# Copying and storing the last left-over rows of a fused attention and feed-forward kernel: two engines with half the columns each, and two stores of 64 rows in place of four of 32

## The chip, the cores and the metric

The kernel runs on one core of one Trainium2 chip. The metric is the device time of one execution in microseconds (us), as a median over runs. A core has a matrix engine (PE, with its weight loads as PEld), VectorE (DVE), ScalarE (ACT), GpSimd (POOL) and SyncE (SP). Transfers between the core's memory and the chip's main memory are issued from an engine's instruction queue and carried out by 16 DMA engines.

## The reference

Eight batches, 8 heads, 576 tokens, head size 64, 32 memory slots; the tokens then go through two dense layers with an ELU between them.

```python
a = exp(phi - max(phi, axis=2)); a = a / (sum(a, axis=2) + 1e-9)
k_m = einsum('bhsm,bhsd->bhmd', a, k)          # 32 slots per head
v_m = einsum('bhsm,bhsd->bhmd', a, v)
attn = softmax(q @ k_m.T / 8)                   # over the 32 slots
x = (attn @ v_m) as [4608 tokens, 512]
h = x @ w_in                                    # 512 -> 2048
g = where(h > 0, h, exp(min(h, 0)) - 1)
out = g @ w_out                                 # 2048 -> 512, all float32
```

## The kernel before

Batches are worked on one after another; a batch's 576 tokens are cut into two halves of 288. The first dense layer (`hidden`, L776) makes, for one of 16 blocks of 128 hidden channels, the channels of one half. ScalarE and VectorE apply the ELU and split the result into a high and a low part. The second layer (`project`, matmuls at L837) multiplies these parts with the weights and sums them in accumulators of 128 tokens by 512 outputs, one bank each (`pso...`).

288 tokens are two full tiles of 128 and 32 left over. The left-over tokens of the two halves of two batches, 4 x 32 = 128, are gathered in tiles called `rest` and go through the second layer together, once for every pair of batches: `rest_high` (ScalarE, L881), `rest_low` (VectorE, L886) and `rest_project` (matmuls, L837), eight steps each. There are four pairs, so this happens four times, and the fourth time is the end of the program.

The order of the work is an explicit list of steps with places; at the end of the last batch the list reads: the last `project`, the eight steps of the left-over tokens with the last two full tiles copied out by `collect` (ScalarE L867, VectorE L869) between them, `store` of these two full tiles (issued on SP, L872), and then `rest_store` of the fourth pair, to which nothing comes after. In `rest_store` ScalarE copies the accumulator of 128 rows by 512 outputs into a tile `orest` (L900), and four transfers bring its rows to the output (L904). Row `n * 32 + i` of the tile is left-over token `i` of batch `2p + n // 2`, half `n % 2`. For the fourth pair the transfers are issued from SP (n = 0 and 2) and from ScalarE's queue (n = 1 and 3). The output is laid out as batch, half, token in half, 512 numbers; the left-over tokens of one half are 32 neighbouring rows there, and those of the next half begin 288 rows further on.

The two full tiles of a half are stored by one transfer whose loops are 128 rows, 2 tiles and 512 numbers (256 rows of 2 KB); a store of left-over rows before has loops of 32 rows and 512 numbers (32 rows of 2 KB).

Of the kernel before, what the change touches and what calls it, by code (L numbers as in the profile page):

```python
# [16 lines left out]
P = 128  # L17
B, H, S, D, M = 8, 8, 576, 64, 32
DM, DFF = 512, 2048
HALF = S // 2  # L20
NT = HALF // P
REST = HALF - NT * P
# [146 lines left out]
def fused_kernel(ctx: ExitStack, tc: tile.TileContext, phiT, phi, kv0, kvt, kv, q0, q1, w_in, w_out, out):  # L169
# [8 lines left out]
    nc = tc.nc  # L178
# [13 lines left out]
    def t2k(shape, name):  # L192
        return work.tile(shape, F32, name=name, tag="t2k", bufs=7)
# [638 lines left out]
    acc = {}  # L832
# [64 lines left out]

    def rest_store(p):
        t = t2k([P, DM], "orest")
        nc.scalar.copy(t, acc.pop(("rest", p)))  # L900

        eng = (nc.sync, nc.scalar) if p == B // 2 - 1 else (nc.sync, nc.sync)
        for n in range(4):
            eng[n % 2].dma_start(  # L904
                out[2 * p + n // 2, n % 2, NT * P :], t[n * REST : (n + 1) * REST, :]
            )

    tiny = work.tile([P, 1], F32, name="tiny", bufs=1)
    warm = ps_o.tile([P, P], F32, name="pso00")
# [4 lines left out]
    def warm_up(n):  # L914
# [8 lines left out]
        for f in (  # L923
# [4 lines left out]
            softmax_divide, back, turn_back, probs_high, probs_low, vw, vw_high, vw_low, hidden,  # L928
            elu_exp, elu_max, elu_rest, rest_copy, elu_high, elu_low, project, collect, store, rest_high, rest_low,
            rest_project, rest_store,  # L930
        )
    }
# [67 lines left out]
    for it, (b, hf, j) in enumerate(order):  # L1000
        at(it - 1.7, hidden, it)
        at(it - 1.69, elu_exp, it)
        at(it - 1.68, elu_max, it)
        if b < NB:
            at(it - 1.67, rest_copy, it)
        elif b > NB and b % 2 == 0 and order[max(it - 2, 0)][0] != b:
            at(32 * b - 0.34 + 0.005 * (it - 32 * b), elu_rest, it)
        else:
            at(it - 1.67, elu_rest, it)
        late = 0.695 if it and b != order[it - 1][0] and b % 2 == 0 and b > NB else 0  # L1010
        at(it - 1 + late, elu_high, it)
        at(it - 0.99 + late, elu_low, it)
        at(it + 0.6, project, it)
        if ends[it][2]:
            for t in range(NT):
                at(it + 0.7, collect, it, t)
            if j == NJ - 1:
                at(it + 0.8, store, b, hf)
                if b % 2 and hf:
                    for i in range(NJ // 2):  # L1020
                        at(it + 0.61 + 0.01 * i, rest_high, b // 2, i)
                        at(it + 0.611 + 0.01 * i, rest_low, b // 2, i)
                        at(it + 0.612 + 0.01 * i, rest_project, b // 2, i)
                    at(it + 0.81, rest_store, b // 2)
# [51 lines left out]
```

## Time and profile before

| what | value |
|---|---|
| median of 3 runs | 713.0 us (712.86 to 714.35) |
| the profiled execution's own time | 713.61 us |
| its span, first to last instruction | 711.8 us |
| PE busy in the span | 700.6 us (98%) |
| DVE busy | 449.1 us (63%) |
| ACT busy | 458.9 us (64%) |
| written to main memory | 9.44 MB |

The span is what the trace sees; the execution's own time is 1.8 us longer. The share of busy time of an engine says how full it is over the whole span, not which engine sets the end: that is read from the chain of work that ended last, and from the last few us in order of time.

### The profile page before, as it was taken

The numbers are of one execution on the slowest core, as the hardware profiler recorded it, in microseconds if no ns is written. First come the engines' busy times: TensorE is split into PE (matmuls) and PEld (weight loads), VectorE is DVE, ScalarE is ACT, GpSimd is POOL, SyncE is SP. The second block draws the span as 40 slices with busy tenths as digits, with TensorE's granted clock in tenths as the row PEclk, the third lists the DMA queues.
The fourth block names the chain that finished last, engine by engine and source line by source line (L and its number), as shares of the span: only waits on it lengthen the run. The fifth ranks groups of instructions, "written<-read, shape, count | busy, mean of one in ns | idle before, by whom it ended". The sixth has DMA issues, their size and how long they took to land.

```text
span 711.8 us, 13641 instructions
## 1 busy us (share of the span) xinstructions
PE 700.6 (98%) x5112; PEld 581.9 (82%) x5112; DVE 449.1 (63%) x1197; ACT 458.9 (64%) x1106; POOL 67.5 (9%) x110
## 2 busy tenths in 40 slices
PE   8899999999999999999999999999999999999997
PEld 7788787878777887788787887888878788778886
DVE  3989788876685459563863638754683546944442
ACT  3888988886456556574664845765574655756652
POOL 1233321323000100010000100001000020000000
PEclk9999999999999999999999999999999999999999
DMA  8991012342303600262003620135001450000001
GB/s 330 407 380 61 1 60 89 112 160 48 134 36 85 200 30 2 97 163 76 1 1 111 164 76 1 49 106 151 31 1 45 92 184 31 1 31 1 29 1 46
DMA packets 25106, 64.46 MB, mean 91 GB/s; under 512 B 3408, under 2 KB 7632, under 8 KB 25040
## 3 DMA queue, kind: packets, MB, share of 16 engines
q1 hardware_dynamic: 24944, 63.46, 27.5%
q8 instruction: 41, 0.67, 0.4%
q14 instruction: 25, 0.20, 0.1%
q10 hardware_dynamic: 96, 0.13, 0.1%
HBM read 54.13 MB, written 9.44 MB: 89 GB/s over the span
## 4 chain that ended last, share of the span: by engine, by line
PE 94%; DVE 2%; DMA 1%; ACT 1%; SPq 1%; issue 0%
PE pso L837 56%; PE psh L776 29%; PE psb L554 4%; PE psb L487 2%; PE pso L554 2%; DMA qh<-q 1%; PE pso L567 1%; PE psb L567 0%; SPq L309 0%; ACT gf L792 0%; PE psb L523 0%; DVE gf L800 0%; ACT gf L791 0%; DVE mx L612 0%; DVE A L713 0%; DVE spare L628 0%
## 5 line engine op out<-in xcount | busy, mean ns | idle before, releaser
L837 PE MATMUL pso<-wout,gp 128*128 128x512 f32 x1728 | 441.0, 395 | 0.5 <-ACT orest L900 0.5
L837 PEld LDWEIGHTS pso<-wout,gp 128*128 128x128 f32 x1728 | 310.7, 188 | 62.4 <-ACT gf L792 2.4
L776 PEld LDWEIGHTS psh<-A,vw 128*128 128x128 f32 x1536 | 227.4, 188 | 36.8 <-issue 11.6
L776 PE MATMUL psh<-A,vw 128*128 128x288 f32 x1536 | 246.5, 297 | 2.2 <-DVE A L713 0.8
L803 DVE SCALAR_TENSOR_TENSOR gf<-gf,psh 128x256 f32<-128x256 f32 x192 | 80.7, 420 | 143.5 <-ACT gf L792 143.3
L791 ACT ACTIVATE gf<-psh 128x288 f32<-128x288 f32 x256 | 104.6, 409 | 103.2 <-PE psh L776 102.3
L823 ACT CAST gp<-gf 128x256 fp32r<-128x256 f32 x256 | 102.9, 404 | 78.2 <-DVE gf L803 66.0
L829 DVE TENSOR_TENSOR gp<-gf,gp 128x256 fp32r<-128x256 f32 x256 | 110.9, 436 | 49.7 <-ACT gp L823 48.6
L792 ACT ACTIVATE gf<-gf 128x288 f32<-128x288 f32 x256 | 113.9, 445 | 8.1
L285 POOL TENSOR_TENSOR e<-e,nmb 128x512 f32<-128x512 f32 (+1 forms) x18 | 21.1, 1198 | 366.5 <-DMA nmb<-nmd 280.6
L800 DVE SCALAR_TENSOR_TENSOR gf<-gf,psh 128x288 f32<-128x288 f32 x64 | 28.6, 451 | 22.0 <-ACT gf L792 21.0
L811 DVE SCALAR_TENSOR_TENSOR rest<-gf,psh 128x32 f32<-128x32 f32 x192 | 34.7, 181 | 0.0
L738 DVE TENSOR_TENSOR vw<-psb,vw 128x512 fp32r<-128x512 f32 (+2 forms) x48 | 27.0, 586 | 3.7 <-ACT vw L732 3.7
L881 ACT CAST gp<-rest 128x256 fp32r<-128x256 f32 x32 | 12.6, 405 | 23.7 <-PE pso L837 23.7
L819 POOL COPY rest<-gf 128x32 f32<-128x32 f32 x64 | 19.1, 329 | 74.0 <-DVE gf L800 73.9
L732 ACT CAST vw<-psb 128x512 fp32r<-128x512 f32 (+2 forms) x48 | 22.5, 497 | 2.5 <-PE psb L554 2.4
L886 DVE TENSOR_TENSOR gp<-rest,gp 128x256 fp32r<-128x256 f32 x32 | 13.0, 418 | 16.3 <-ACT gp L881 16.3
L554 PE MATMUL psb<-win,kvm 64*32 64x512 f32 (+2 forms) x384 | 22.3, 521 | 0.0
L383 ACT ACTIVATE mag<-raw 128x512 uint32<-128x512 uint32 x30 | 19.9, 669 | 1.7 <-DVE top L405 1.7
L379 ACT ACTIVATE mag<-raw 128x512 f32<-128x512 f32 x30 | 19.9, 668 | 0.0
L738 DVE TENSOR_TENSOR vw<-pso,vw 128x512 fp32r<-128x512 f32 (+1 forms) x28 | 17.3, 626 | 0.0
L487 PE MATMUL psb<-kvt,e 128*32 128x128 f32 (+1 forms) x480 | 15.1, 274 | 0.0
(133 smaller groups left out, 438.1 us busy)
## 6 DMA issues: line engine op xcount, KB each, us to landing
kvt<-kv SPq DMA_DIRECT2D x32, 512.0 KB, 7.5
raw<-w_in SPq DMA_DIRECT2D x15, 512.0 KB, 9.9
raw<-w_out SPq DMA_DIRECT2D x15, 512.0 KB, 4.2
out<-osb SPq DMA_DIRECT2D x14, 512.0 KB, 2.8
qt<-q SPq DMA_DIRECT2D x18, 384.0 KB, 4.1
ph<-phiT SPq DMA_DIRECT2D x7, 576.0 KB, 4.6
e<-phi SPq DMA_DIRECT2D x12, 256.0 KB, 4.7
kvt<-kv SPq DMA_DIRECT2D x6, 256.0 KB, 10.0
```

Of the source, the lines that this page charges most:

```text
L487: nc.tensor.matmul((ps[a] if b < NB else ps[:, a])[32 * j : 32 * j + 32], s["e"][c // 2][rows, c % 2, x : x + M], kv_rows(b, c, i, 2 * j + a),
L554: nc.tensor.matmul(outs[a][32 * j : 32 * j + 32, :], lhs[r, 32 * j : 32 * j + 32], rhs[r, j], start=True, stop=True, tile_position=(64 * a ...
L738: nc.vector.tensor_tensor(t[:, LO, a, n0:n1], s["ps"]["vw", c, n0][a], t[:, HI, a, n0:n1], ALU.subtract)
L776: nc.tensor.matmul(ps, t[:, x, g, c0 : c0 + P], s["A"][hf][:, y, g, :], start=(n == 0), stop=(n == 5),)
L791: nc.scalar.activation(gf, ps, AF.Relu, scale=-1.0)
L792: nc.scalar.activation(gf, gf, AF.Exp, scale=-1.0)
L800: nc.vector.scalar_tensor_tensor(gf, gf, -1.0, ps, ALU.add, ALU.max)
L803: nc.vector.scalar_tensor_tensor(gf[:, :n], gf[:, :n], -1.0, ps[:, :n], ALU.add, ALU.max)
L811: nc.vector.scalar_tensor_tensor(rest_of(b, j)[:, o : o + REST], gf[:, n:], -1.0, ps[:, n:], ALU.add, ALU.max)
L823: nc.scalar.copy(gp[:, HI], gs[it][:, : NT * P])
L829: eng.tensor_tensor(gp[:, LO], gf[:, : NT * P], gp[:, HI], ALU.subtract)
L837: nc.tensor.matmul(ps, gp[:, y], wout[j][:, x, :], start=(first and n == 0), stop=(last and n == 2),)
```

## The change

Only the fourth `rest_store` is changed; the first three pairs keep one copy on ScalarE and four transfers on SP. For the fourth pair ScalarE copies columns 0 to 255 of the accumulator and VectorE columns 256 to 511, and two transfers follow, one from SP with the rows of batch 6 and one from ScalarE's queue with those of batch 7. Each takes 64 rows of the tile and writes them as 2 halves by 32 rows by 512 numbers.

```diff
     def rest_store(p):
         t = t2k([P, DM], "orest")
-        nc.scalar.copy(t, acc.pop(("rest", p)))
-
-        eng = (nc.sync, nc.scalar) if p == B // 2 - 1 else (nc.sync, nc.sync)
-        for n in range(4):
-            eng[n % 2].dma_start(
-                out[2 * p + n // 2, n % 2, NT * P :], t[n * REST : (n + 1) * REST, :]
-            )
+        ps = acc.pop(("rest", p))
+        if p < B // 2 - 1:
+            nc.scalar.copy(t, ps)
+            for n in range(4):
+                nc.sync.dma_start(
+                    out[2 * p + n // 2, n % 2, NT * P :], t[n * REST : (n + 1) * REST, :]
+                )
+            return
+        nc.scalar.copy(t[:, : DM // 2], ps[:, : DM // 2])
+        nc.vector.tensor_copy(t[:, DM // 2 :], ps[:, DM // 2 :])
+        for n, eng in enumerate((nc.sync, nc.scalar)):
+            eng.dma_start(out[2 * p + n, :, NT * P :], t[n * 2 * REST : (n + 1) * 2 * REST, :])
```

How the instructions stand on ScalarE at the end of the program, lines of before with a minus and of the change with a plus. In brackets are the counters that an instruction waits for: those of PE, DVE and Activation (ScalarE) count finished work of that engine, and DMAHW0 to DMAHW7 count transfers.

```order
 L881 CAST gp<-rest 128x256 [waits DVE_49,PE_49] x6
 L867 COPY osb<-pso_7875 128x512 [waits DMAHW6_49]
-L900 COPY orest<-pso_8174 128x512 [waits PE_49]
-L904 DMA out<-orest 32x512 [waits DMAHW1_49,Activation_49]
-L904 DMA out<-orest 32x512 [waits DMAHW3_49]
-L1071 UNCONDITIONAL_BRANCH
+L908 COPY orest<-pso_8174 128x256 [waits PE_49]
+L911 DMA out<-orest 2x32x512 [waits DMAHW1_49,DVE_49]
+L1076 UNCONDITIONAL_BRANCH
```

The copy has half the columns, one transfer of loops 2 x 32 x 512 stands where two of 32 x 512 stood, and it waits for VectorE's counter and no longer for ScalarE's own.

On VectorE, at the end of the program:

```order
 L886 TENSOR_TENSOR gp<-rest,gp 128x256 [waits Activation_49] x8
 L869 COPY osb<-pso_7876 128x512 [waits DMAHW6_49]
-L1071 UNCONDITIONAL_BRANCH
+L909 COPY orest<-pso_8174 128x256 [waits Activation_49]
+L1076 UNCONDITIONAL_BRANCH
```

VectorE's copy is new there, and it waits for ScalarE's counter, not for PE's. The value that it waits for is the count that ScalarE reaches with its own half of the copy.

On SP, at the end of the program:

```order
 L872 DMA out<-osb 128x2x512 [waits DMAHW7_49,DVE_49,Activation_49]
 L872 DMA out<-osb 128x2x512 [waits DMAHW0_49,DVE_49,Activation_49]
-L904 DMA out<-orest 32x512 [waits DMAHW2_49,Activation_49]
-L904 DMA out<-orest 32x512 [waits DMAHW4_49]
-L1071 UNCONDITIONAL_BRANCH
+L911 DMA out<-orest 2x32x512 [waits DMAHW2_49,DVE_49]
+L1076 UNCONDITIONAL_BRANCH
```

SP issues one transfer after VectorE's copy where it issued two after ScalarE's. The loops shown are those of the written side; on the side of the tile the transfer has one loop of 64 rows.

## Rows read from the trace of the kernel before

**Rows 1.** The page: the span, the busy time of each engine with its share and count of instructions, and, in 40 equal slices of the span, the busy tenths of PE and the granted clock of TensorE in tenths.

```profile
span 711.8 us, 13641 instructions
PE 700.6 (98%) x5112; PEld 581.9 (82%) x5112; DVE 449.1 (63%) x1197; ACT 458.9 (64%) x1106; POOL 67.5 (9%) x110
...
PE   8899999999999999999999999999999999999997
...
PEclk9999999999999999999999999999999999999999
```

**Rows 2.** The chain of work that ended last, the pieces from 690 us on, in order of time: start us, us, what.

```profile
692.57 15.09 PE pso L837 x66
707.65 0.02 issue
707.68 0.58 ACT orest L900
```

**Rows 3.** The instructions from 705 us to the end in order of time: start us, us, engine (SPq and ACTq are the instruction queues, where transfers are issued), line, operation, tiles, count, and in brackets the idle time before it and what ended it.

```profile
704.32 0.68 DVE L869 COPY osb<-pso 128x512 f32<-128x512 f32 x1
704.71 2.93 PE L837 MATMUL pso<-wout,gp 128*128 128x512 f32 x12
...
705.07 0.37 SPq L872 DMA_DIRECT2D out<-osb  x1
707.68 0.58 ACT L900 COPY orest<-pso 128x512 f32<-128x512 f32 x1 [3.25 <-PE pso L837]
708.29 0.80 SPq L904 DMA_DIRECT2D out<-orest  x2
708.29 0.87 ACTq L904 DMA_DIRECT2D out<-orest  x2
```

**Rows 4.** Who waited for whom on SP's queue from 690 us on: us in total, times, longest. L1071 is the end of the program.

```profile
SPq L1071 <- DMA out<-orest: 1.6, 1, 1.6
```

**Rows 5.** Groups of instructions by line and shape, whole span: line, engine, operation, out<-in, shapes and count, then busy us, mean ns of one, and idle us before them. Copies out of an accumulator bank with 512 and with 256 columns, on ScalarE and on VectorE.

```profile
L900 ACT COPY orest<-pso 128x512 f32<-128x512 f32 x4 | 2.3, 582 | 7.0 <-PE pso L837 7.0
L532 ACT COPY kvm<-psb 128x256 f32<-128x256 f32 x6 | 2.1, 358 | 1.4 <-PE psb L523 1.4
L471 ACT COPY win<-pso 128x256 f32<-128x256 f32 x1 | 0.4, 354 | 0.0
L471 DVE COPY spare<-psb 128x256 f32<-128x256 f32 x1 | 0.4, 424 | 0.5 <-PE psb L462 0.5
```

**Rows 6.** Instructions around 703.5 us in order of time, columns as in rows 3: a VectorE instruction that waits for one of ScalarE.

```profile
703.53 0.41 ACT L881 CAST gp<-rest 128x256 fp32r<-128x256 f32 x1 [0.98 <-PE pso L837]
...
703.98 0.42 DVE L886 TENSOR_TENSOR gp<-rest,gp 128x256 fp32r<-128x256 f32 x1 [0.96 <-ACT gp L881]
```

**Rows 7.** The transfer issues on SP around 398.4 and 399 us, columns as in rows 3. The first row is two loads of 128 rows of 4 KB, the second is one of 128 rows and one of 64 rows.

```profile
398.36 0.86 SPq L299 DMA_DIRECT2D kvt<-kv  x2
...
398.84 1.02 SPq L299 DMA_DIRECT2D kvt<-kv  x2
```

**Rows 8.** DMA traffic from 709 to 709.44 us: the busy share in tenths of the 16 DMA engines, in 40 slices of 0.011 us, and the packets of each queue (q1 holds the transfers issued on SP, q10 those issued on ScalarE's queue): packets, MB, share.

```profile
DMA  0000000000099908605970990099998000740609
...
q1 hardware_dynamic: 35, 0.06, 59.1%
q10 hardware_dynamic: 1, 0.00, 2.0%
```

**Rows 9.** DMA traffic from 710 us to the end of the span, in 40 slices of 0.05 us: busy tenths of the 16 engines.

```profile
DMA  9595100000000000000000000000000000000000
```

**Rows 10.** DMA traffic from 705.5 to 708 us, in which only the store of the two full tiles (L872, 256 rows of 2 KB) runs: packets, MB; then how many of them are under 512 bytes, under 2 KB and under 8 KB.

```profile
DMA packets 272, 0.52 MB, mean 210 GB/s; under 512 B 16, under 2 KB 16, under 8 KB 272
```

**Rows 11.** DMA traffic from 709 to 710.5 us, in which only the four stores of left-over rows (L904, 32 rows of 2 KB each, two from each queue) run.

```profile
DMA packets 192, 0.26 MB, mean 175 GB/s; under 512 B 64, under 2 KB 64, under 8 KB 192
...
q10 hardware_dynamic: 96, 0.13, 37.9%
q1 hardware_dynamic: 96, 0.13, 29.9%
```

**Rows 12.** Three stretches: us, busy time of PE, PEld, DVE, ACT and POOL, granted TensorE clock, mean busy share of the 16 DMA engines, GB/s. The first lies in the store of the two full tiles, the second and third in the stores of left-over rows.

```profile
706.40:706.90 0.50, 0.50 (x4) 0.41 (x3) 0.00 (x0) 0.00 (x0) 0.00 (x0) 1.00 0.98 389
709.40:709.70 0.30, 0.00 (x0) 0.00 (x0) 0.00 (x0) 0.00 (x0) 0.00 (x0) 1.00 1.02 219
709.70:710.00 0.30, 0.00 (x0) 0.00 (x0) 0.00 (x0) 0.00 (x0) 0.00 (x0) 1.00 0.91 308
```

## The prediction

> **What bounds the kernel now.** I read the page first. PE is busy for 98% of the span at full granted clock [rows 1], so nothing that another engine saves counts before PE's last matmul. The edit lies wholly behind that matmul. The second view is therefore the chain that ended last, in order of time: a run of matmuls up to 707.65 us, then ScalarE's copy of the left-over accumulator [rows 2], to which no other work runs beside on PE, DVE or ACT [rows 3]. From there on everything is serial and uncovered: copy, issue, transfer, end of program. A us gained or lost in it is a us of the kernel.
>
> The third view is the end in order of time. The copy ends at 707.68 + 0.58 = 708.26; both queues begin to issue at 708.29, two transfers each [rows 3]. The first data of SP's transfers moves at 709.12 (the twelfth slice of 0.011 us) and ScalarE's at 709.44, where its queue has one packet [rows 8]: 0.83 and 1.15 us after the issue began. The last data is through at 710.3 [rows 9]. The wait that ends last is SP's, at the end of the program, for these stores [rows 4]. From the last data to the end of the span, 711.8 - 710.3 = 1.5 us go into the landing's report and the closing of the program. So the tail of 4.15 us behind PE is: copy 0.6, issue to first data 0.85, data 1.2, closing 1.5.
>
> **The change, part by part.**
>
> The copy. ScalarE's half is the same operation as the 256-column copies out of a bank, 0.354 to 0.358 us [rows 5], so it ends at 707.68 + 0.36 = 708.04. VectorE's half doesn't run beside it: as it stands on its queue it waits for ScalarE's count, not PE's. Such a handover takes 703.98 - 703.94 = 0.04 us [rows 6]. VectorE's 256-column copy is 0.424 us [rows 5], so it ends at 708.04 + 0.04 + 0.42 = 708.50, where before the whole copy was done at 708.26. Halved and serial, the copy costs 0.24 us more. Nothing is queued behind the waiting copy but the end of the program; both stores wait for it. Were the halves side by side, they would end at 707.68 + 0.42 = 708.10, 0.16 us sooner than before.
>
> The issues. Each queue now issues once. Before, the second issue of a queue went on while the data of the first was on its way, so removing it takes at most the 0.4 us by which it stood behind the first [rows 3]. The new issue has a form that the trace doesn't show; the nearest is a 64-row load on SP, which took 0.16 us longer to issue than a 128-row one (1.02 for the pair against 0.86) [rows 7]. I take 0.15, with 0 and 0.3 as ends. First data: SP 708.52 + 0.83 + 0.15 = 709.50, ScalarE's queue 708.52 + 1.15 + 0.15 = 709.82.
>
> The data. The bytes are the same, 128 rows of 2 KB. What is in question is over how many DMA engines they are dealt. The trace allows a count: a transfer leaves small packets of a few bytes behind its rows, 272 - 256 = 16 for the store of the full tiles [rows 10], and 192 - 128 = 64 for the four stores of 32 rows [rows 11], 16 for each. With 16 engines on the core the plain reading is one for each engine that took part. So stores whose outer loop has 128 or 32 steps on both sides, each divisible by 16, were dealt over all 16. The new store has an outer loop of 2 on the written side and of 64 on the tile's side; the pieces that both have in common are 2, each of 32 rows. If work is dealt out by pieces of the outer loops, each store runs on 2 engines. No row of this trace has such a pair of loops, so both ends must be kept: 16 engines, or 2. I take 2, since in each store counted the outer loops match and divide by 16, and here they do neither. The Trainium skill, DMA: Bandwidth & Descriptors, section on why a DMA increments its semaphore by 16, gives the count as the largest up to 16 that divides the slowest dimension of both sides, and says that such a transfer takes the lowest-numbered engines; it would be 2 here, the same two for both stores. The trace agrees as far as its 16 small packets go, and no run so far shows a smaller count.
>
> With the same two engines for both stores, each has 64 rows, one after another. The price of a row on one engine is read from the rate and the share [rows 12]. In the store of the full tiles 389 GB/s at a share of 0.98 is 24.8 GB/s for a busy engine: 83 ns for 2 KB. In the stores of left-over rows it was 219 GB/s at 1.02, 13.4 GB/s, 153 ns, while both queues were at rows of the first half of the tile, and 308 at 0.91, 21.2 GB/s, 97 ns, once rows of the other half joined in. Ends: 64 x 83 = 5.3 us and 64 x 153 = 9.8 us. The new stores have rows of the first half on SP and of the second on ScalarE's queue, both at once, and are nearest to the third stretch: 64 x 97 = 6.2 us. The Trainium skill, SBUF, section Door 1, has a reason for the slow rate: partitions p and p + 32 share a port, so a transfer from partitions 0 to 63 has half the ports; that would put the two engines of one store on one port, and by its 27.2 GB/s a port I'd estimate 4.8 us with two ports always busy and 9.6 us with one.
>
> **The sum.** The data runs from 709.50 to 709.50 + 6.2 = 715.7, where it ended at 710.3: +5.4 us. Copy and issue are in that start. The closing 1.5 us stays. The span becomes 711.8 + 5.4 = 717.2 and the profiled execution's own time 713.61 + 5.4 = 719.0. It was 0.6 above the median of the runs, so for the median I take 713.0 + 5.4 = 718.4 us. With the ends of the row's price: +4.5 (717.5) and +9.0 (722.0).
>
> **The rivals.**
>
> *Sixteen engines anyway (not slower).* The hardware may see that 2 x 32 rows on the written side are the 64 on the tile's side and deal by rows. Then each engine has 8 rows: 4 from 709.50 on and 4 from 709.82 on, done between 709.82 + 4 x 0.097 = 710.2 and 709.50 + 8 x 0.153 = 710.7, against 710.3: -0.1 to +0.4 us, and the time is 713.0 to 713.4. The saved issue and the serial copy cancel. For it: every transfer counted so far used all 16; against it: each had matching outer loops. It decides wherever a store is dealt over 8 engines or more: at 8 the data is 16 x 0.097 = 1.6 us, and the loss 0.8 us.
>
> *Two engines, other ones for each store.* Then an engine has 32 rows, from 709.82 on for the later store: 32 x 0.083 to 32 x 0.153 is 2.7 to 4.9 us, ending at 712.5 to 714.7: +2.2 to +4.4 us, 715.2 to 717.4. Both queues reaching all 16 engines in the stores before (16 small packets for each) speaks against it.
>
> *The two engines in step.* If both keep to the same half of the tile at any moment, the slow stretch's 153 ns holds throughout: +9.0, 722.0 us. For it: both engines start one store together. Against: two queues feed each engine, and in the third stretch mixed rows came at 97 ns.
>
> *Faster.* What the edit can save at all is 0.16 us of copy if the halves ran together and 0.4 of issue, 0.6 us or 0.08%; it can't reach the 0.2% below.
>
> **How the numbers follow.** The measurement tells from no change what differs by more than about 0.2%, 1.4 us. Chances: 0.55 for two shared engines near the row's middle price, 0.18 for them in step, 0.08 for separate pairs, 0.17 for sixteen engines, 0.02 for gains that I see no source of. Slower: 0.55 + 0.18 + 0.08 = 0.81; same 0.17; faster 0.02. The range takes in the first three cases, 0.81: from 715.2 (separate pairs at the lowest price) to 722.0 + 0.3 for the issue + 0.3 for spread between runs, 722.6. The likeliest case's own range is 717.2 to 720.
>
> **What would show it.** The chain to PE's last matmul is as before and ends near 707.7. VectorE's L909 starts about 0.04 us behind ScalarE's L908, which takes 0.36. Both queues issue once, near 708.5. In the stretch of the stores the small packets number 4 and not 32, DMA's share is about 2/16 = 0.12 and the rate 40 to 50 GB/s, for 6 us. SP's wait for the stores, 1.6 us before, grows to some 7. It is wrong if 32 small packets show, if the share stands at 0.8 or more, or if the data is through before 711 us.

## The result and the profile after

| what | before | change |
|---|---|---|
| median of 5 runs | 713.14 us | 721.03 us (719.86 to 722.44) |
| ratio, with its 95% interval | 1 | 1.0087 (1.0063 to 1.0111) |
| span of the profiled execution | 711.8 us | 720.7 us |
| from the end of PE's last matmul to the end of the span ("the tail") | 4.15 us | 10.8 us |

The change makes the kernel slower by 0.87%, or 6.2 us by the ratio; the range ran from 715.2 to 722.6 us, and the forecast was 718.4. The two medians lie further apart, 7.9 us, and PE doesn't end at the same time in every execution, as two profiles of the change below show; the tail leaves that out.

The end of the chain that ended last, in the profile of the change (start us, us, what), answers to [rows 2]:

```profile
694.79 15.09 PE pso L837 x66
709.87 0.02 issue
709.89 0.38 ACT orest L908
710.28 0.02 issue
710.30 0.42 DVE orest L909
```

PE's last 66 matmuls take the same 15.09 us, and VectorE's half of the copy follows ScalarE's. PE ends at 709.87 where it ended at 707.65, 2.2 us later. That part isn't the edit's, as the lines below say (busy times of the engines from 20 to 40 us, then the granted clock, the DMA share and the rate; first this profile, with five of these 20 us by themselves, then a second one of the same kernel, from the last run below).

```profile
20.00:40.00 20.00, 18.39 (x191) 15.78 (x192) 16.54 (x41) 15.35 (x36) 4.62 (x3) 0.83 1.02 406
25.00:30.00 5.00, 5.00 (x44) 4.33 (x44) 3.65 (x10) 3.32 (x9) 2.84 (x2) 0.50 1.03 407
```

```profile
20.00:40.00 20.00, 18.19 (x235) 14.88 (x233) 19.08 (x47) 17.66 (x44) 5.04 (x5) 1.00 1.02 406
```

In the first profile TensorE's granted clock was 0.83 in the mean of this stretch and 0.50 from 25 to 30 us, which is 1.2 GHz in place of 2.4, some 670 us ahead of the edit. In the second it had the full clock, PE ended at 707.83, and the span was 718.6: 6.8 us over that of before, nearly all of it tail. So all profiles below are compared by their tails.

The issues of the change, in order of time (columns as in [rows 3]):

```profile
710.75 0.67 SPq L911 DMA_DIRECT2D out<-orest  x1
710.76 1.38 ACTq L911 DMA_DIRECT2D out<-orest  x1
```

DMA traffic of the change from 711 us to the end (packets, MB; then those under 512 bytes, 2 KB and 8 KB; then the two queues), which answers to [rows 11]:

```profile
DMA packets 132, 0.26 MB, mean 27 GB/s; under 512 B 4, under 2 KB 4, under 8 KB 132
...
q1 hardware_dynamic: 66, 0.13, 5.7%
q10 hardware_dynamic: 66, 0.13, 3.5%
```

The 128 rows left 4 small packets where before they left 64. Each store now leaves 2: two engines each. Two stretches of these stores (columns as in [rows 12]):

```profile
712.00:715.20 3.20, 0.00 (x0) 0.00 (x0) 0.00 (x0) 0.00 (x0) 0.00 (x0) 0.76 0.12 29
716.80:718.80 2.00, 0.00 (x0) 0.00 (x0) 0.00 (x0) 0.00 (x0) 0.00 (x0) 0.50 0.13 51
```

Two of 16 engines is a share of 0.125, and that is the share in both. A busy engine moves 29 / (16 x 0.12) = 15.1 GB/s in the first, 136 ns for a row of 2 KB, and 24.5 GB/s in the second, 84 ns. The shares of the two queues above are of 16 engines over 9.7 us: on average 138 ns for a row of SP's store and 85 ns for one of ScalarE's. The packets of the queues from 711 to 715.2 us, and then from 715.2 to 716 us:

```profile
q1 hardware_dynamic: 46, 0.09, 9.3%
```

```profile
q1 hardware_dynamic: 9, 0.02, 9.8%
q10 hardware_dynamic: 5, 0.01, 3.3%
```

46 rows of SP's queue moved by 715.2 us and none of ScalarE's, which had been issued at 710.76. ScalarE's first rows came right after that, while SP's still had 18 to go. The wait for the stores at the end of the program (us in total, times, longest) was 1.6 us before [rows 4]:

```profile
SPq L1076 <- DMA out<-orest: 8.2, 2, 5.7
```

### The profile page after: what moved, and what is told of

Same layout as the page of the kernel before. It is cut to its first block, busy times and chain, and to the rows that moved or that the text cites. A ratio compares the mean times of both kernels' runs of the same rounds, so it can differ in the third digit from the quotient of the medians.

```text
span 720.7 us, 13640 instructions
## 1 busy us (share of the span) xinstructions
PE 704.0 (98%) x5112; PEld 584.8 (81%) x5112; DVE 452.4 (63%) x1198; ACT 459.0 (64%) x1106; POOL 67.9 (9%) x110
## 4 chain that ended last, share of the span: by engine, by line
PE 94%; DVE 1%; DMA 1%; ACT 1%; SPq 0%; issue 0%
PE pso L837 56%; PE psh L776 29%; PE psb L554 4%; PE psb L487 2%; PE pso L554 2%; DMA qh<-q 1%; PE pso L567 1%; PE pso L921 1%; ACT gf L792 0%; ACT gf L791 0%; PE psb L567 0%; SPq L309 0%; PE psb L523 0%; ACT win L471 0%; PE psh L670 0%
## 5 line engine op out<-in xcount | busy, mean ns | idle before, releaser
L829 DVE TENSOR_TENSOR gp<-gf,gp 128x256 fp32r<-128x256 f32 x256 | 113.6, 446 | 49.7 <-ACT gp L823 48.6
L738 DVE TENSOR_TENSOR vw<-pso,vw 128x512 fp32r<-128x512 f32 (+1 forms) x28 | 17.2, 623 | 0.0
L921 PE MATMUL pso<-ident 128*128 128x128 f32 x84 | 15.2, 352 | 1.6 <-POOL ident masks.py:199 1.6
```

The lines of the kernel that those rows point to most:

```text
L738: nc.vector.tensor_tensor(t[:, LO, a, n0:n1], s["ps"]["vw", c, n0][a], t[:, HI, a, n0:n1], ALU.subtract)
L829: eng.tensor_tensor(gp[:, LO], gf[:, : NT * P], gp[:, HI], ALU.subtract)
```

## The experiments

All are told by their tail as well as by their time. The ratio is to before, with its 95% interval, where a run was timed in rounds. Medians of before in these sessions were 714.0 to 715.0 us, so times are compared by their ratio. Diffs are against the change; where they show added lines alone, these stand in place of the copies and stores of the last pair.

### Each half of the change alone

Halved copies, with the four stores of before:

```diff
         nc.scalar.copy(t[:, : DM // 2], ps[:, : DM // 2])
         nc.vector.tensor_copy(t[:, DM // 2 :], ps[:, DM // 2 :])
-        for n, eng in enumerate((nc.sync, nc.scalar)):
-            eng.dma_start(out[2 * p + n, :, NT * P :], t[n * 2 * REST : (n + 1) * 2 * REST, :])
+        for n in range(4):
+            (nc.sync, nc.scalar)[n % 2].dma_start(
+                out[2 * p + n // 2, n % 2, NT * P :], t[n * REST : (n + 1) * REST, :]
+            )
```

> Half of the change alone: ScalarE and VectorE copy half the columns each, and the four stores of 32 rows stay. Theory (the stores are dealt over two engines, and that is the whole loss): the time is that of before plus 0.2 to 0.3 us for the second half waiting for the first, 713.2 to 713.5 us; the tail behind PE's last matmul is 4.4 us (4.15 before, 10.8 with the change), with 64 small packets behind the rows. Rival (the copy on two engines and its wait cost most of it): a tail above 8 us and 717 us or more.

Measured: ratio 1.0007 (0.9993 to 1.0022), a tail of 714.5 - 710.1 = 4.4 us. The copies and SP's issues, in order of time:

```profile
710.15 0.37 ACT L908 COPY orest<-pso 128x256 f32<-128x256 f32 x1 [3.25 <-PE pso L837]
710.56 0.42 DVE L909 COPY orest<-pso 128x256 f32<-128x256 f32 x1 [3.08 <-ACT orest L908]
711.01 0.80 SPq L911 DMA_DIRECT2D out<-orest  x2
```

The packets of the stores (here and below: all packets, MB, and those under 512 bytes, 2 KB and 8 KB):

```profile
DMA packets 192, 0.26 MB, mean 75 GB/s; under 512 B 64, under 2 KB 64, under 8 KB 192
```

The copy is 0.25 us longer, and that is the whole difference of the tail to before. The copies are not the cause.

Whole copy, with the two stores of the change:

```diff
-        nc.scalar.copy(t[:, : DM // 2], ps[:, : DM // 2])
-        nc.vector.tensor_copy(t[:, DM // 2 :], ps[:, DM // 2 :])
+        nc.scalar.copy(t, ps)
```

> The other half of the change alone: ScalarE copies all columns, and two stores of 64 rows follow. Theory: 4 small packets, a DMA share near 0.12, data for 6.5 to 7.5 us, a tail of 10.4 to 10.6 us (that of the change less the 0.24 of the serial copies), 719 to 721 us. Rival (the copies): 713 us and 64 or 32 small packets.

Measured: ratio 1.0088 (1.0066 to 1.0110), a tail of 717.9 - 707.3 = 10.6 us. SP's wait for the stores (us in total, times, longest) and their packets:

```profile
SPq L1075 <- DMA out<-orest: 8.3, 2, 5.8
```

```profile
DMA packets 132, 0.26 MB, mean 25 GB/s; under 512 B 4, under 2 KB 4, under 8 KB 132
```

The loss is in the stores.

### The outer loop of the written side: 4, 32, and 24 with 8

One copy, and one store of all 128 rows as 4 blocks of 32 rows:

```diff
+        nc.scalar.copy(t, ps)
+        nc.sync.dma_start(
+            out[2 * p : 2 * p + 2, :, NT * P :].rearrange("b h s x -> (b h) s x"), t
+        )
```

> One copy on ScalarE, and one store of all 128 rows from SP, whose loops on the written side are 4 blocks of 32 rows. Theory: work is dealt by the outer loop, so 4 engines take part with 32 rows each and 4 small packets are left; first data near 709.5, 32 rows at 84 to 153 ns are 2.7 to 4.9 us, so a tail of 6.0 to 8.3 us and 715.0 to 717.2 us, between before and the change. Rival (any store of more than 32 rows or of this form of issue falls to two engines): 2 small packets and 64 rows an engine, 718 us or more. Rival (the number of engines doesn't matter, two queues at once do): the data moves in about 1 us, 713 us.

Measured: ratio 1.0035 (1.0021 to 1.0049), a tail of 715.0 - 707.4 = 7.6 us. SP's wait and the packets:

```profile
SPq L1076 <- DMA out<-orest: 5.2, 1, 5.2
```

```profile
DMA packets 132, 0.26 MB, mean 37 GB/s; under 512 B 4, under 2 KB 4, under 8 KB 132
```

One store, 4 small packets: 4 engines (a share of 0.25 of 16, shown further down), and a tail between the two kernels.

The same, with the rows in the tile by token first. The tile's rows are the columns of `rest`, so only where VectorE writes them changes, for the last pair alone:

```diff
+        to = rest_of(b, j)[:, o : o + REST]
+        if b // 2 == B // 2 - 1:
+            to = rest_of(b, j).rearrange("p (s n) -> p n s", n=4)[:, b % 2 * 2 + hf, :]
...
+        nc.sync.dma_start(
+            out[2 * p : 2 * p + 2, :, NT * P :].rearrange("b h s x -> s (b h) x"), t
+        )
```

> As the run with one store of 128 rows, but the left-over rows of the last pair stand in the tile by token first (row 4 * token + batch and half), so that the loops on the written side are 32 tokens by 4 rows: the outer loop divides by 16. Theory: 16 engines with 8 rows each and 16 small packets, data for 0.7 to 1.2 us from 709.3 to 709.6 on, a tail of 3.6 to 4.3 us, 712.5 to 713.2 us: all of the loss gone, with one store of 128 rows. Rival (the loss comes from one large store, or from its longer issue, not from dealing): as the run with 4 blocks, 715 us or more.

Measured: ratio 1.0000 (0.9986 to 1.0014), a tail of 715.0 - 710.9 = 4.1 us. SP's wait and the packets:

```profile
SPq L1077 <- DMA out<-orest: 1.8, 1, 1.8
```

```profile
DMA packets 144, 0.26 MB, mean 75 GB/s; under 512 B 16, under 2 KB 16, under 8 KB 144
```

The same bytes, one store of the same size from the same queue: with an outer loop of 32 in place of 4 it runs on 16 engines, and the tail is that of before. So neither the size of a store nor the form of its issue is the cause.

Then that store cut into 24 and 8 tokens, both from SP:

```diff
+        to = out[2 * p : 2 * p + 2, :, NT * P :].rearrange("b h s x -> s (b h) x")
+        for a, z in ((0, 24), (24, 32)):
+            nc.sync.dma_start(to[a:z], t[4 * a : 4 * z, :])
```

> As the run with the rows by token and one store of 128 rows, but cut into two stores from SP whose outer loops are 24 and 8 tokens (by 4 rows): both divide by 8 and not by 16. Theory of dealing by the outer loops: 8 small packets for each store, 12 and then 4 rows for each of 8 engines; by the 121 ns a row of a lone store over two engines, or 84 at best, the first store's rows take 1.0 to 1.5 us from 1.3 us after the issue on, and the tail is 4.6 to 5.4 us, between that of 16 engines (4.1) and of 4 (7.6). Rival (only an outer loop of less than the engines, 2 or 4, is dealt badly): 16 small packets for the store of 24.

Measured, in one execution: a tail of 715.7 - 710.6 = 5.1 us, and the count:

```profile
DMA packets 148, 0.26 MB, mean 52 GB/s; under 512 B 20, under 2 KB 20, under 8 KB 148
```

The tail is as expected, the count is not: 20 small packets, where two stores on 8 engines leave 16 and the rival would have left 24. 20 is 12 + 8, and 12 is the largest number up to 16 that divides 24 and the tile's 96 rows; my expectation had overlooked it. A stretch of the first store agrees (columns as in [rows 12]): its share of 0.69 is more than 8 of 16 engines can give, 0.50, and near the 0.75 of 12.

```profile
713.00:713.60 0.60, 0.00 (x0) 0.00 (x0) 0.00 (x0) 0.00 (x0) 0.00 (x0) 1.00 0.69 181
```

That an outer loop of 24 beside one of 96 gives 12 is the rule of the Trainium skill, DMA: Bandwidth & Descriptors, section on why a DMA increments its semaphore by 16, to the letter; with it stand the counts of 2, 4 and 16 above.

### The change as it is, with the outer loop repaired

Halved copies and two stores of 64 rows from two queues, as in the change, but with the tile's rows as 64 * batch + 2 * token + half:

```diff
-            eng.dma_start(out[2 * p + n, :, NT * P :], t[n * 2 * REST : (n + 1) * 2 * REST, :])
+            eng.dma_start(
+                out[2 * p + n, :, NT * P :].rearrange("h s x -> s h x"),
+                t[n * 2 * REST : (n + 1) * 2 * REST, :],
+            )
```

> The change with its two copies and its two stores of 64 rows from the same queues, but the left-over rows of the last pair stand as 64 * batch + 2 * token + half, so that the loops on the written side are 32 tokens by 2 halves. Theory of dealing: 16 engines and 16 small packets for each store, data done about 1 us after the first row, and nearly all of the loss gone: a tail of 4.2 to 4.8 us (serial copies 0.25, longer issue 0.4, one issue less), 713 to 713.6 us where nothing else disturbs. Rival (two stores of 64 rows at once are slow whatever their loops): a tail above 8 us.

Measured: ratio 0.9995 (0.9978 to 1.0013), a tail of 712.3 - 707.7 = 4.6 us. The issue on ScalarE's queue, in order of time, and the packets of both stores:

```profile
708.60 0.65 ACTq L912 DMA_DIRECT2D out<-orest  x1
```

```profile
DMA packets 160, 0.26 MB, mean 75 GB/s; under 512 B 32, under 2 KB 32, under 8 KB 160
```

16 engines for each store, and 6.2 of the 6.65 us are gone. What is left is 0.45 us over before; the serial copy is 0.25 of it, and the rest is not taken apart here.

### Why the data took 7.4 us and not 6.2

The change with each store taking every second row of the tile, so that its two engines read rows of different halves (VectorE writes the left-over rows in the matching order):

```diff
-            eng.dma_start(out[2 * p + n, :, NT * P :], t[n * 2 * REST : (n + 1) * 2 * REST, :])
+            eng.dma_start(out[2 * p + n, :, NT * P :], t[n :: 2, :])
```

> The change with its copies and its two stores of 2 x 32 rows, but the left-over rows of the last pair stand in the tile as 2 * (32 * half + token) + batch, and a store takes every second row. So the two engines of a store read rows of different halves of the tile (0 to 62 and 64 to 126), where with the change they read rows p and p + 32 of the same half at the same time. Theory of the in-step price (the rows of 100 to 500 ns come from two engines at rows of one half): the 32 rows an engine of SP's store take 32 x 84 ns = 2.7 us where the change took 4.8, the data in all 5.4 to 6 us, the tail 8.8 to 9.5 us (10.8 with the change). Rival (the slow rows come from elsewhere: the way the rows reach the engines, or the written side): the same as with the change, 10.5 to 11 us. Either way 4 small packets.

Measured: ratio 1.0083 (1.0058 to 1.0108), a tail of 722.4 - 712.4 = 9.9 us. The first part of SP's store (columns as in [rows 12]), and the rows moved from 714 to 716.8 us:

```profile
714.58:716.80 2.22, 0.00 (x0) 0.00 (x0) 0.00 (x0) 0.00 (x0) 0.00 (x0) 0.70 0.13 37
```

```profile
q1 hardware_dynamic: 40, 0.08, 10.4%
```

The tail lies between the two expectations. Again SP's rows go first and alone (40 of them, none of ScalarE's, issued at 713.34). The rate rose from 29 to 37 GB/s, not to the 49 or more of two engines at 84 ns a row. Which half of the tile is read explains 0.9 us at most; by itself it isn't what makes the rows slow. Once ScalarE's rows were there, the two stores did take turns, as the packets from 717.8 to 719.4 us show:

```profile
q1 hardware_dynamic: 20, 0.04, 6.6%
q10 hardware_dynamic: 20, 0.04, 6.6%
```

Twenty rows of each store in 1.6 us, with a share of 0.13 for both together: the same two engines work for both, at 80 ns a row.

A half of the tile read alone isn't slow either. In the run with the outer loop repaired, ScalarE's store has the second half alone; its packets from 710.75 to 710.85 us, when SP's rows were through:

```profile
DMA packets 21, 0.04 MB, mean 410 GB/s; under 512 B 1, under 2 KB 1, under 8 KB 21
...
q10 hardware_dynamic: 21, 0.04, 105.6%
```

A two-engine store beside stores of 32 rows, once from ScalarE's queue, once from SP (edit of the first; the second is its mirror image):

```diff
+        nc.scalar.copy(t, ps)
+        nc.scalar.dma_start(out[2 * p + 1, :, NT * P :], t[2 * REST :, :])
+        for n in range(2):
+            nc.sync.dma_start(out[2 * p, n, NT * P :], t[n * REST : (n + 1) * REST, :])
```

> One copy on ScalarE; ScalarE's queue issues one store of 2 x 32 rows, SP two stores of 32 rows. With the change ScalarE's first row moved 4.5 us after its issue. If it waits there for SP's rows on the same two engines: first row 1.3 to 2.0 us after the issue, 32 rows an engine, 2.7 to 4.9 us of data, a tail of 6.3 to 8.5 us. If ScalarE's queue delivers such a store late by itself: first row 4 us or more after the issue and a tail of 9 us or more. 2 small packets from ScalarE's queue, 32 from SP's.

> The mirror image: SP issues one store of 2 x 32 rows, ScalarE's queue two stores of 32 rows. If the slow rows of SP's store in the change (32 an engine in 4.8 us, 150 ns each) are the store's own, they stay: 4.5 to 5 us of data and a tail of 7.5 to 8.3 us. If they come from the second store being issued beside it: 2.7 to 3 us of data and a tail of 5.5 to 6.3 us.

Measured, one execution each: tails of 715.1 - 707.9 = 7.15 and 715.9 - 708.7 = 7.2 us. For the first, ScalarE's issue, in order of time, and the packets of the two queues from 708.5 to 709.9 us:

```profile
708.56 1.15 ACTq L909 DMA_DIRECT2D out<-orest  x1
```

```profile
q1 hardware_dynamic: 48, 0.07, 19.4%
q10 hardware_dynamic: 1, 0.00, 0.4%
```

For the second, SP's issue, its wait for the stores, and its packets from 709.3 to 714.6 us:

```profile
709.35 0.67 SPq L909 DMA_DIRECT2D out<-orest  x1
```

```profile
SPq L1076 <- DMA out<-orest: 4.8, 1, 4.8
```

```profile
q1 hardware_dynamic: 66, 0.13, 8.2%
```

ScalarE's first row is under way by 709.9, 1.3 us after its issue; in the change it was over 4.4 (none by 715.2). So its queue isn't late by itself: what held it up in the change goes with SP's two-engine store. It was not that SP's rows had to be through first, for 18 of them, and 24 in the run with every second row, were still to come when ScalarE's began. What it was is not shown.

By the packets' times SP's store took 3.9 us from first to last row in the mirror run, 121 ns a row with a few rows of ScalarE's stores between them; by the share above one of its own rows took 109 ns. I had expected 2.7 to 3 us or 4.5 to 5, and it is neither. With the second two-engine store it was 4.8 us, but no run has such a store with nothing beside it. The nearest is the one store over 4 engines, also 32 rows an engine, which took 4.3 us by the packets' times. Two stretches of it:

```profile
709.40:710.80 1.40, 0.00 (x0) 0.00 (x0) 0.00 (x0) 0.00 (x0) 0.00 (x0) 1.00 0.25 19
711.00:713.00 2.00, 0.00 (x0) 0.00 (x0) 0.00 (x0) 0.00 (x0) 0.00 (x0) 0.86 0.25 89
```

All four engines were busy in both, but a row took about 430 ns in the first and 92 ns in the second. So the slow rows stand mostly at the start of a store over few engines, and neither a second store, nor just two engines, nor rows of one half alone are needed for them.

### The change once more

> The change once more, timed in more rounds, and a second profile of it. The tail behind PE's last matmul is 10.8 us again (SP's rows first, 4.8 us, then ScalarE's), whatever TensorE's clock did earlier in that execution; the time is 0.8 to 1.0% above before.

Measured: ratio 1.0090 (1.0068 to 1.0111), a tail of 718.6 - 707.8 = 10.8 us, and SP's wait as in the first profile:

```profile
SPq L1076 <- DMA out<-orest: 8.2, 2, 5.8
```

## Why the prediction was right, point by point

**The chain and where it is uncovered.** Right: nothing behind PE's last matmul hid any of the loss, and the tail grew by 10.8 - 4.15 = 6.65 us, which is what the ratio gives (6.2, with 4.5 to 7.9 in its interval).

**The copy.** Right: 0.37 + 0.04 + 0.42 us, done 0.85 us behind PE's end, as expected, and the run with the copies alone put the price at 0.25 us.

**The issue.** Right in kind, 0.3 us too short: SP's first row moved 1.27 us after the issue began, where I had 0.98 from the longer issue of a 64-row load [rows 7]. The runs with 16 engines have nearly the same (1.3 us), so the price belongs to the form of the transfer, not to its two engines. For ScalarE's queue the step was wrong: its first row was to move 1.30 us after the issue and moved after some 4.5.

**The number of engines.** Right, and the deciding step: 2 for each store, and the same two for both, as the share of 0.13 with rows of both stores moving shows (the run with every second row). The counts of small packets in the runs, 2, 4, 12 + 8, 16, and their tails of 10.8, 7.6, 5.1 and 4.1 us follow the outer loop with bytes unchanged. The row counts in the profile of before [rows 10, 11] were enough to see how to count engines, and not enough to see the rule.

**The price of a row.** This term was mis-sized: 64 rows an engine in 7.4 us (712.0 to 719.4), 115 ns a row, where I took 97 ns and 6.2 us; the mean rate was 36 GB/s, where I had 40 to 50. The step that failed is the reason given for it: that rows of both halves would be moved side by side from the start, as in the third stretch of [rows 12], and that a row's price hangs on which halves are read. For 3.2 us SP's rows moved alone, at 136 ns; ScalarE's came after that, and took 85 ns on average. And rows of one half alone moved at 410 GB/s over 16 engines, so the 153 ns of the second stretch isn't the price of one half. That 97 ns came near the mean of slow first rows and fast later ones is in part luck.

**The sum.** 5.4 us were predicted. The later first row adds 0.3 and the slower rows 1.2, and the closing is 0.2 us shorter (1.26 for 1.48 us, for a reason that no run shows): 6.7, as measured by the tail. By the tail the likeliest case's own range, up to 720 us, holds; the median of 721.03 us lies above it, since it also holds what differs between executions ahead of the edit.

**The rivals.** *Sixteen engines anyway* fell with 4 small packets in place of 32. *Other engines for each store* fell with the share, 0.12 to 0.13 also where rows of both stores move, and not 0.25. *The two engines in step* was priced at 153 ns for all rows; the mean was 115, and moving the two engines to different halves of the tile left SP's rows slow (37 GB/s), so its mechanism was not the cause, or not alone. *Faster*: with the stores repaired the tail is 4.6 us against 4.15, so there was nothing to gain even then.

**Open.** Why the rows of a store over few engines mostly come slowly at first and at 84 ns later is not settled. It is not which half of the tile they are read from, and it is there in a store over four engines with nothing beside it; where the rows are written was not varied. Nor is it settled why ScalarE's first row came 4.5 us after its issue.

No version beat before: the best, one store by token, ended 4.1 us behind PE against 4.15, which no timing here can tell apart.

## What to carry to other kernels

Before two transfers are merged into one, look at the outermost loop on both sides, as the transfer is issued: in all runs here the largest number up to 16 that divides both was the number of engines that worked on it, so 2 blocks of 32 rows go over two engines and 32 rows of 2 go over sixteen. If the blocks can't be moved on the written side, reorder the rows where they are produced. At the very end of a program nothing hides such a store, and the count of small packets behind it says in one line of the profile how many engines it had.

## What the runs showed of the hardware that I had not expected

- Of two stores over the same two engines, issued within 0.01 us of each other from two queues, the second came late: none of ScalarE's rows had moved when 46 of SP's 64 had, although a two-engine store from ScalarE's queue beside stores over 16 engines began 1.3 us after its issue. Once both had rows to move, the engines took them in turn (20 and 20 in 1.6 us).
- The first rows of a store over four engines took about 430 ns each with every engine busy, the later ones 92 ns.
- The issue itself got longer: ScalarE's queue spent 1.38 us on one two-engine store (0.65 for the same rows dealt over 16), SP 0.67.
- 24 tokens of 4 rows went over 12 engines, not 8.
- Early in some executions, of the change and of others, TensorE's granted clock fell to its lower level for a time (0.83 in the mean from 20 to 40 us in the change's first profile, after 20 us with PE busy for 17.2) and PE ended 2.2 us later. The second profile of the same kernel has 1.00 there, so it came and went between executions.
